# Convolution in two token halves, with the feed-forward of the first half interleaved, in a fused layer kernel

## The chip, the core and the metric

The kernel runs on one core of a Trainium2 chip. Its time is the device time of one execution in microseconds (us); the smaller, the better. A core has five engines that run their own instruction queues in order and meet only through semaphores: PE (TensorE, matrix products), ACT (ScalarE), DVE (VectorE), POOL (GpSimd) and SP (SyncE, which here issues nearly all DMAs). Matmul results land in PSUM, eight banks per partition, and have to be copied out ("evicted") to SBUF by ACT or DVE.

## The reference

Shapes: S = 2048 tokens, D = 640 channels, F = 1728 hidden features, bfloat16.

```python
k_shift = sum over t of k_pad[:, t:t + S, :] * shift_k[:, ks - 1 - t]      # 4 taps
kv = k_shift * v
y  = irfft(rfft(kv, 2S) * rfft(ssm_k, 2S))[:S] + kv * ssm_D                # causal, per channel
h  = x + layernorm(x) * y                                                  # x is A_q
h2 = h + (mish(layernorm(h) @ w1 + b1)) @ w2
```

Mish is h * tanh(softplus(h)). So there is a causal convolution over 2048 tokens in each channel, two layer norms, a gate and a feed-forward of 640 to 1728 to 640.

## The kernel before

**The convolution.** The transform of length 4096 is done as products on PE. Time is split as t = 16 t1 + t2. *Stage 1* (`stage1`, L500, matmuls L510 and L511) multiplies, for each group of channels, a 128 x 64 slice with a cosine and a sine table of 128 columns; the two write the two halves of the partitions. *Stage 2* (`s2_pe`, L527, matmul L539) has one 128 x 128 table per frequency f1 (128 of them, tile G), times 64 or 32 columns. Both run once for the filter (names s1k, s2k) and once for kv (s1v, s2v). G is not loaded: a compact table R (1 MB) is loaded (L473) and DVE spreads it by 16 masked products (`gb`, L483).

The filter is transposed on PE first (k1, L560). The shift with its four taps runs as small matmuls with diagonal matrices on 32 rows each (kspe, L586), from k loaded by transposing DMAs (d_kT, L476); DVE multiplies the result with v (L597). The filter's spectrum KP is also copied with the partition halves exchanged, by 20 DMAs of 256 KB (d_swap, L639), so that the complex product is two element-wise products on DVE (L720). The *inverse* is two steps: i1 (L731 and L732, two accumulating products per group, 20 evictions) and i2 (L782, six matmuls for a tile of 128 tokens, all 128 rows and columns in use).

**The rest.** For each of 16 token tiles: statistics of x (L676, L677), a reciprocal root on POOL (L422), the normalised x on ACT (lnx, L789), times the convolution out of PSUM (wb, L793), plus x (h, L797), statistics of h (L802, L803), the normalised h (dr, L812), five PE transposes (trpe, L819) and their eviction (trev). A unit of tokens (UNITS: 128, 128, 256, 512, 512, 512) then goes through the first product (m1pe, L845, 14 feature chunks of 128, the last half empty), Mish on ACT (hb, L851), the second product (m2pe, L861, 28 matmuls a tile), the addition of h (res, L870) and the output DMA (L873). Up to 24 filler matmuls (L830) keep PE running between i1 and the first unit.

**What sets the order.** The program lists operations with costs, dependences and priorities (table PRIO); `_schedule` (L145) plays them out on model engines, chooses ACT or DVE for each eviction and a pair of PSUM banks, and the instructions are emitted in the order of the modelled start. The evictions go through one helper, `ev` (L388; ACT is L390, DVE is L392). The feed-forward waits for the whole convolution: every i2 tile reads all of i1's output, and i1 comes after all products.

Of the kernel before, what the change touches and what calls it, by code (L numbers as in the profile page):

```python
# [11 lines left out]
ALU = mybir.AluOpType  # L12
# [4 lines left out]
S = 2048  # L17
# [4 lines left out]
NDG = 160  # L22
# [3 lines left out]
UNITS = [128, 128, 256, 512, 512, 512]  # L26
CHAIN = [80, 80.5, 81, 81.5] + [100.3, 100.31, 101.3, 101.31] + [102.3, 102.31, 102.32, 102.33] + [103.3, 103.31, 103.32, 103.33]
GRP_DC = [[0, 1], [2, 3], [4]]
GRP_DG = [(32 * g[0], 32 * g[-1] + 32) for g in GRP_DC]
NGRP = len(GRP_DC)  # L30
Q_KN = ("sp",) * NDC
Q_R = "sp"
Q_V = "sp"
Q_SWAP = "sp"
KTP = 16 + S
PRIO = {
    "k11": -197.031, "kv3": -192.001, "trev5": -189.16, "dr4": -188.917, "ln1_4": -185.4, "d_w2_8": -183.299, "i2pe1": -183.28, "d_w1_1": -182.827,
    "ln2s_14": -182.817, "ln1_11": -182.369, "ln1_13": -179.511, "wb7": -178.983, "dr0": -177.34, "lnx8": -174.207, "s1v4": -173.982,
    "ln1_9": -173.036, "ln1_15": -173.036, "h12": -173.025, "dr14": -173.025, "dr9": -172.894, "s2k0": -172.418, "ln2_15": -172.408, "h13": -172.023,
    "d_x1": -171.432, "ln2s_12": -170.801, "gb3": -167.776, "ln1_10": -166.532, "trpe6": -166.522, "trpe3": -165.629, "h11": -164.77,  # L40
    "ln2_0": -158.964, "kv2": -157.471, "s2k1": -157.461, "d_w1_4": -157.461, "ln1f6": -140.087, "d_kn0": -136.228, "h14": -87.6278, "h5": -84.944,
    "d_kn1": -84.3457, "h3": -84.0417, "wb11": -83.75, "dadd2": -79.55, "prod1": -75.932, "s1v3": -71.4952, "i2pe0": -68.0843, "ln1_6": -65.6205,
    "d_small": -63.7909, "i2pe3": -46.3801, "prod0": -44.976, "h1": -43.6934, "kv1": -39.0187, "ln1_14": -38.1351, "ln2_11": -38.1251,
    "lnx11": -36.0598, "d_R": -35.7363, "dadd0": -33.0275, "i2pe5": -33.0079, "wb1": -30.0642, "k10": -28.9847, "i2pe2": -28.8839, "h10": -28.7223,
    "d_t2m2": -27.8175, "kv4": -26.7596, "ks2": -24.7067, "kTpad": -24.6967, "trpe14": -18.2332, "ln2s_2": -18.2232, "ln1_8": -16.2738,
    "s2v1": -13.55, "wb14": 53.9493, "dr2": 56.1891, "trev11": 76.4003, "prod2": 76.4103, "trev2": 76.5744, "lnx12": 83.0874, "ln1f12": 84.6952,
    "ln2s_7": 84.9682, "i2pe7": 85.4105, "s1k1": 85.8777, "ln1s4": 86.1434, "lnx13": 86.1434, "ln2s_13": 86.1434, "d_w2_2": 86.2865, "wb12": 86.3538,
    "wb6": 88.7157, "trev9": 88.8047, "dr1": 89.3089, "h2": 90.4433, "dadd3": 91.1611, "lnx15": 91.1711, "d_x2": 91.1811, "wb10": 96.232,
    "trpe0": 97.2334, "d_w2_6": 97.2434, "gb2": 99.9385, "dadd4": 100.943, "c_diag": 102.191, "ln1_12": 103.577, "i10": 103.587, "s2v2": 103.597,
    "h8": 103.597, "lnx10": 103.607, "d_kn3": 104.126, "wb2": 106.246, "trpe2": 107.085, "h7": 107.848, "ln2_5": 107.903, "i2pe6": 108.973,  # L50
    "dr10": 110.068, "d_t2m3": 110.222, "k14": 111.266, "d_x3": 111.276, "ln2s_5": 111.611, "lnx4": 111.807, "d_b1": 112.158, "h4": 112.585,
    "s1k3": 112.595, "k13": 113.424, "dr15": 113.55, "ln2_13": 114.336, "i12": 114.475, "wb5": 114.476, "i2pe4": 114.485, "d_x0": 115.118,
    "d_w2_12": 115.124, "trev14": 115.124, "lnx9": 115.128, "lnx2": 115.378, "d_w1_0": 115.411, "trev12": 115.469, "ln1_5": 115.479, "ln1f0": 115.674,
    "d_w2_4": 115.88, "ln1s0": 116.071, "ln2s_11": 116.442, "d_kn4": 116.478, "ks3": 116.488, "s1k4": 116.498, "s1v2": 116.498, "trpe1": 116.508,
    "trev4": 116.686, "dr13": 117.267, "dr12": 117.27, "lnx3": 117.281, "ln2s_10": 118.476, "ln1f2": 120.706, "ln2s_4": 121.167, "trpe5": 121.177,
    "ln2_14": 121.46, "trev1": 121.47, "ln1s2": 121.577, "ln1f4": 121.587, "d_kn2": 122.535, "dr3": 123.819, "trev6": 124.987, "h6": 125.859,
    "ln2s_3": 126.587, "ln1f8": 126.597, "s2v0": 126.931, "ks0": 126.987, "d_v1": 127.413, "ln2_6": 127.672, "i2pe8": 127.672, "dr6": 127.682,
    "trev15": 128.067, "gb0": 128.252, "ln2_2": 129.397, "h0": 129.422, "dr5": 129.653, "dr11": 130.28, "ln2_3": 130.769, "wb15": 130.779,
    "gb1": 130.789, "d_v0": 132.33, "trev0": 132.596, "ln2_7": 133.484, "i2pe11": 135.983, "ln1s12": 137.388, "ln2s_9": 137.679, "ln2_1": 139.461,
    "d_t2m0": 140.202, "trpe7": 140.669, "kv0": 142.766, "trev13": 142.775, "ln2s_15": 144.326, "ks1": 144.336, "ln2s_1": 144.482, "ln2_8": 145.614,  # L60
    "trpe15": 145.919, "k12": 145.929, "dr8": 149.209, "lnx7": 150.735, "d_w2_10": 150.975, "trev8": 150.985, "wb4": 151.881, "trpe8": 152.822,
    "c_b1": 153.173, "s1k0": 154.561, "d_kT0": 155.252, "trev3": 155.262, "d_w1_3": 155.316, "dadd1": 155.326, "s1v1": 155.326, "trpe4": 155.336,
    "ln2_10": 155.388, "d_x6": 155.398, "ln1s8": 156.048, "ln1_1": 156.058, "lnx1": 156.078, "d_x7": 157.931, "ln1_3": 159.901, "d_swap2": 160.38,
    "wb0": 160.441, "i2pe9": 160.974, "d_x5": 160.984, "i2pe12": 163.067, "ln2s_6": 163.441, "d_kT1": 164.275, "trpe10": 165.151, "i2pe13": 167.089,
    "ln2_4": 169.091, "i2pe10": 169.366, "trpe13": 170.057, "wb13": 170.931, "ln1_0": 172.475, "trpe12": 172.485, "ln1_7": 172.852, "i2pe15": 173.706,
    "ln2s_8": 174.688, "trpe9": 175.572, "d_w1_2": 176.078, "i2pe14": 176.088, "trev10": 177.413, "ln2_9": 179.75, "s2k2": 181.125, "d_t2m1": 181.135,
    "dr7": 183.042, "s1v0": 184.508, "wb3": 187.188, "d_kT4": 193.464, "d_w2_0": 195.652, "s1k2": 196.175, "ks4": 196.195, "ln1s6": 198.464,
    "ln2s_0": 199.521, "ln2_12": 199.531, "trev7": 201.426, "i11": 202.634, "h9": 202.644, "d_kT2": 204.785, "d_x4": 207.553, "d_swap0": 209.773,
    "h15": 210.788, "wb8": 214.107, "lnx14": 217.331, "ln1_2": 217.341, "lnx5": 217.861, "lnx0": 219.423, "d_kT3": 222.092, "lnx6": 223.895,
    "trpe11": 227.243, "wb9": 230.005, "d_swap1": 230.845,  # L70
}

OFF_KP = 0
OFF_KPS = 40960
OFF_KN = OFF_KPS
OFF_KT = OFF_KN + 20480
OFF_G = OFF_KT + NDC * KTP * 2
OFF_B = OFF_G + 32768
OFF_V = OFF_B + 40960
OFF_KK = OFF_V + 20480  # L80
OFF_XA = OFF_KK + 8192
OFF_KVB = OFF_XA + 8192
OFF_END = OFF_KVB + 12288
OFF_KVB2 = OFF_KK
OFF_R = OFF_XA
OFF_W1 = OFF_G
OFF_W2 = OFF_KPS
OFF_LNHT = OFF_KP
OFF_UB0 = OFF_KP + 20480
OFF_UB1 = OFF_KPS + 17920  # L90
OFF_T2M = OFF_KVB
OFF_LNX = OFF_KVB + 8192
OFF_HC = OFF_XA
OFF_OB = OFF_XA + 3840

class _Ring:


# [3 lines left out]
_CELL = {}  # L102
# [8 lines left out]

class _Op:
    __slots__ = ("name", "opts", "deps", "allocs", "emit", "prio", "lat", "start", "finish", "eng", "done", "picks", "cap", "xbar")

    def __init__(self, name, opts, deps, allocs, uses, emit, prio, lat):
        self.name = name
        self.opts = opts if isinstance(opts, list) else [opts]
        self.deps = deps
        self.allocs = list(allocs)
        for rt in list(allocs) + list(uses):  # L120
            rt.users.append(self)
        self.emit = emit
        self.prio = prio
        self.lat = lat
        self.start = None
        self.finish = None
        self.eng = None
        self.done = False
        self.cap = 0.0
        self.xbar = False  # L130

_WIN = 0.3
_SEM = 0.18
_OWN = {"act": 0.1, "dve": 0.1}
_FIRST = 0.6
_LAST_BYTE = 1.6

def _stage(name):
    m = re.match(r"(k1|s1k|s2k|kp|ks|kv|s1v|s2v|x|prod|i1|gb|d_swap|c_diag|d_kn|d_kT|d_R|d_v)(?:pe|ev)?(\d*)(?:_.*)?$", name)
    if not m:  # L140
        return name
    st = {"kp": "s2k", "x": "s2v"}.get(m.group(1), m.group(1))
    return st + m.group(2)

def _schedule(ops):  # L145
    _CELL.clear()
    free = {}
    order = []
    cap_free = 0.0
    ring_free = {}  # L150
    ring_sent = {}
    ndeps = {id(o): len(o.deps) for o in ops}
    children = {}
    for o in ops:
        for d in o.deps:
            children.setdefault(id(d), []).append(o)
    bl = {}
    for o in reversed(ops):
# [768 lines left out]
```

## Time and profile before

| what | value |
|---|---|
| median of 3 runs | 244.1 us (242.97 to 246.27) |
| profiled execution, first to last instruction (the page names no other time of it) | 238.7 us |
| PE busy | 221.0 us (93%), 3266 matmuls |
| VectorE busy | 155.5 us (65%) |
| ScalarE busy | 139.5 us (58%) |
| GpSimd busy | 20.3 us (9%) |
| DMA | 25.52 MB, mean 107 GB/s |
| granted TensorE clock | 1.000 |

A row of busy time adds what an engine ran, overlaps within the engine counted once. In the rows of groups, "xN" is the number of instructions, "128x1024 bf16<-128x1024 f32" the output and the input (partitions x elements, type). The chain of waits is followed back from the last instruction; the timeline has start, duration, engine, line and operation, with the idle time before it in brackets. The largest groups are the evictions on ACT (L390, 78 of 1024 elements, 73.2 us), the second product (L861, 62.0 us) and the first (L845, 62.3 us). Matmuls are pipelined: the mean duration of one (L861: 299 ns) is longer than the distance from one to the next.

### The profile page before, as it was taken

How to read it: one execution, taken by the hardware profiler on the slowest of the kernel's cores; microseconds unless marked ns; L12 is line 12 of the kernel's file. 1: busy time of each engine (PE TensorE's matmuls, PEld its weight loads, DVE VectorE, ACT ScalarE, POOL GpSimd, SP SyncE). 2: the span in 40 equal slices, each digit the busy share in tenths (PEclk: the TensorE clock that was granted, in tenths of full speed). 3: DMA queues.
4: the chain of work that ended last, by engine and by line, in shares of the span. 5: the costliest groups of instructions: out<-in, count | busy, mean ns of one | idle time of the engine just before them, and what ended most of it. 6: DMA issues, size and time to landing. Idle time of an engine off the chain costs nothing.

```text
span 238.7 us, 7414 instructions
## 1 busy us (share of the span) xinstructions
PE 221.0 (93%) x3266; PEld 167.2 (70%) x3266; DVE 155.5 (65%) x318; ACT 139.5 (58%) x192; POOL 20.3 (9%) x39
## 2 busy tenths in 40 slices
PE   8888688988779999999999999999999999999993
PEld 3777577888779998698788764577744677545772
DVE  0998967899979998899999898584350332100121
ACT  2668676989998999589166456930156401366000
POOL 2500000000000003022311200210000000000000
PEclk9999999999999999999999999999999999999999
DMA  6999999806999797000000000001000001000001
GB/s 235 393 340 228 173 181 225 124 3 150 238 233 388 236 368 292 5 3 3 27 30 1 27 30 0 0 4 55 27 30 0 0 30 52 31 0 3 27 27 55
DMA packets 20049, 25.52 MB, mean 107 GB/s; under 512 B 11633, under 2 KB 15538, under 8 KB 19634
## 3 DMA queue, kind: packets, MB, share of 16 engines
q1 hardware_dynamic: 19760, 24.88, 37.5%
q8 instruction: 25, 0.41, 0.7%
q10 hardware_dynamic: 146, 0.18, 0.5%
q0 software_dynamic: 112, 0.01, 0.1%
q14 instruction: 6, 0.05, 0.1%
HBM read 14.57 MB, written 2.62 MB: 72 GB/s over the span
## 4 chain that ended last, share of the span: by engine, by line
PE 77%; ACT 10%; issue 4%; DVE 4%; DMA 3%; SPq 0%; ACTq 0%; DVEq 0%
PE banks L861 26%; PE banks L845 25%; ACT arena L390 9%; PE banks L539 6%; PE banks L731 4%; PE banks L732 4%; PE banks L782 3%; DMA arena<-tab_R 3%; PE banks L510 3%; PE banks L586 2%; DVE arena L392 2%; PE banks L819 2%; PE banks L560 1%; PE banks L830 1%; PE banks L511 1%
## 5 line engine op out<-in xcount | busy, mean ns | idle before, releaser
L390 ACT CAST arena<-banks 128x1024 bf16<-128x1024 f32 x78 | 73.2, 1046 | 16.3 <-PE banks L511 10.6
L845 PE MATMUL banks<-arena 128*128 128x512 bf16 (+2 forms) x420 | 62.3, 308 | 0.3 <-ACT arena L390 0.2
L861 PE MATMUL banks<-arena 128*128 128x320 bf16 x448 | 62.0, 299 | 0.2 <-DVE arena L793 0.2
L851 ACT ACTIVATE arena<-banks,b1s 128x512 bf16<-128x512 f32 (+2 forms) x84 | 43.5, 546 | 27.6 <-PE banks L845 25.5
L861 PEld LDWEIGHTS <-arena 128*128 128x128 bf16 x448 | 43.6, 98 | 17.1 <-issue 0.4
L845 PEld LDWEIGHTS <-arena 128*128 128x128 bf16 x420 | 35.3, 98 | 25.7 <-issue 0.7
L870 DVE TENSOR_TENSOR arena<-banks,arena 128x640 bf16<-128x640 f32 x16 | 13.2, 824 | 43.3 <-PE banks L861 43.2
L539 PE MATMUL banks<-arena 128*128 128x64 bf16 (+1 forms) x768 | 25.3, 188 | 4.6 <-ACT arena L390 2.9
L392 DVE CAST arena<-banks 128x1024 bf16<-128x1024 f32 x22 | 26.3, 1221 | 4.5 <-PE banks L511 2.2
L390 ACT COPY arena<-banks 128x640 bf16<-128x640 bf16 (+1 forms) x12 | 8.6, 746 | 32.7 <-PE banks L819 32.5
L539 PEld LDWEIGHTS <-arena 128*128 128x128 bf16 x768 | 23.3, 97 | 6.2 <-issue 5.1
L720 DVE TENSOR_TENSOR arena<-arena 128x1024 bf16<-128x1024 bf16 x40 | 24.8, 687 | 2.2 <-ACT arena L390 1.7
L510 PE MATMUL banks<-consts,arena 128*64 128x128 bf16 x320 | 21.3, 220 | 3.4 <-ACT arena L390 2.0
L511 PE MATMUL banks<-consts,arena 128*64 128x128 bf16 x320 | 21.6, 221 | 0.0
L511 PEld LDWEIGHTS <-arena 128*64 128x64 bf16 x320 | 18.4, 110 | 3.4 <-issue 3.2
L731 PE MATMUL banks<-consts,arena 128*128 128x128 bf16 x160 | 18.8, 219 | 1.3 <-DVE arena L392 0.9
L510 PEld LDWEIGHTS <-arena 128*64 128x64 bf16 x320 | 18.7, 110 | 1.7 <-issue 1.0
L732 PE MATMUL banks<-consts,arena 128*128 128x128 bf16 x160 | 18.7, 219 | 0.0
L732 PEld LDWEIGHTS <-arena 128*128 128x128 bf16 x160 | 15.6, 98 | 1.3 <-issue 1.0
L731 PEld LDWEIGHTS <-arena 128*128 128x128 bf16 x160 | 15.6, 98 | 0.6 <-issue 0.6
L789 ACT ACTIVATE arena<-arena,nmr_75,r1v 128x640 bf16<-128x640 bf16 x16 | 14.4, 926 | 2.6 <-DVE nmr_75 L684 1.4
L392 DVE COPY arena<-banks 128x1024 bf16<-128x1024 bf16 (+1 forms) x14 | 8.0, 598 | 11.8 <-PE banks L819 11.7
(47 smaller groups left out, 181.0 us busy)
## 6 DMA issues: line engine op xcount, KB each, us to landing
arena<-arena SPq DMA_DIRECT2D x20, 256.0 KB, 6.0
arena<-in_A_ssm_k_dram SPq DMA_DIRECT2D x5, 512.0 KB, 8.2
arena<-in_A_v_dram SPq DMA_DIRECT2D x2, 1280.0 KB, 15.4
arena<-in_A_q_dram SPq DMA_DIRECT2D x8, 320.0 KB, 5.6
out_dram<-arena SPq DMA_DIRECT2D x16, 160.0 KB, 1.8
arena<-in_B_w_dram SPq DMA_DIRECT2D x5, 432.0 KB, 8.4
arena<-in_B_w_dram SPq DMA_DIRECT2D x6, 320.0 KB, 4.8
arena<-tab_R SPq DMA_DIRECT2D x1, 1024.0 KB, 7.4
```

The lines of the kernel that those rows point to most:

```text
L390: clock.append(nc.scalar.copy(o, i))
L392: nc.vector.tensor_copy(o, i)
L510: nc.tensor.matmul(ps1[0:64, gl, :], lhs, fcfs_b[:, 0, :], start=True, stop=True)
L511: nc.tensor.matmul(ps1[64:128, gl, :], lhs, fcfs_b[:, 1, :], start=True, stop=True)
L539: nc.tensor.matmul(ps2[:, c0:c0 + nd], G_t()[:, f0 + fl, :], src[:, f0 + fl, :], start=True, stop=True)
L720: nc.vector.tensor_tensor(kp, x, kp, ALU.mult)
L731: nc.tensor.matmul(pz[:, gl, :], KP_t()[:, dg, :], a12_b[:, 0, :], start=True, stop=False)
L732: nc.tensor.matmul(pz[:, gl, :], KPS_t()[:, dg, :], a12_b[:, 1, :], start=False, stop=True)
L789: nc.scalar.activation(lnx.tile, xn_t()[:, t2, :], ACT.Identity, scale=r1v[:, t2:t2 + 1], bias=nmr1[:, t2:t2 + 1])
L845: nc.tensor.matmul(ph[:, 0:w], w1_t()[:, dc, fc * P:(fc + 1) * P], lnhT_t()[:, dc, c0:c0 + w], start=(dc == 0), stop=(dc == NDC - 1))
L851: nc.scalar.activation(ub_t[u % 2]()[:, fc, 0:w], rt.tile[:, 0:w], ACT.Mish, bias=b1s[:, fc:fc + 1], scale=1.0)
L861: nc.tensor.matmul(po[:, hf2 * 512:hf2 * 512 + 320], hb[:, fc, tl * P:(tl + 1) * P], w2_t()[:, fc, hf2 * 320:(hf2 + 1) * 320], start=(fc = ...
```

## The change

The file is rewritten in most places. What it does:

- **Two halves.** Tokens are cut in two windows of 1024. The transform has half the length (64 frequencies f1, NF, in place of 128; G has 64 tables). The filter has two windows of its spectrum (KA and KB), kv has two (XA and XB). Half 0 of the output is XA times KA; half 1 is XB times KA plus XA times KB. Stage 2 of the filter handles both windows in one matmul of 128 columns (64 for the last group), that of kv goes window by window (s2v, s2w).
- **Products.** prod (half 0) is one DVE instruction of 2048 elements that reads x twice through a repeated operand. Half 1 takes three such instructions per slice of channels (pu, pt, pa; 10 slices).
- **Swaps.** 10 DMAs of 256 KB for KA, then 40 of 128 KB for half 1's operands (d_swapr, d_swapk).
- **Order.** The feed-forward of tokens 0 to 1023 (units 0 to 4) is emitted between the products and inverse stage of half 1 (pu, pt, pa, i1b). Nine units of 128 or 256 tokens. There is no scheduler any more: `ORDER` is a string of all operations with engine and bank slot, in the order in which they are emitted.
- **i2.** Eight matmuls per tile, each on 64 rows and 64 columns, N = 320. A tile's partitions are two runs of 64 tokens, so x is loaded in 16 DMAs and out is stored in 34.
- **Stage-2 table.** G is loaded from DRAM in four DMAs of 512 KB (2 MB in all); the masked products are gone.
- **Transposes.** Tiles 0 and 1 keep PE transposes; tiles 2 to 15 are transposed by DMA (d_tr, on SP's queue).
- **m1.** In a unit of two tiles the last feature chunk (64 features) takes both tiles side by side on the two halves of the columns. The last tile's second product is split in 512 and 128 columns.
- **Statistics.** The addition of epsilon and the scaling move from DVE to POOL; some of the statistics of x may run on ACT (two activations with a sum), some of dr on ACT.
- **Gone:** fillers, paced DMAs.

The diff, cut to its core:

```diff
-UNITS = [128, 128, 256, 512, 512, 512]
+UNITS = [[0], [1], [2, 3], [4, 5], [6, 7], [8, 9], [10, 11], [12, 13], [14, 15]]
...
+ORDER = """
+d_consts:a d_kn0:s warmset:d d_small:v d_kn1:s pewarm:p:0 d_kn2:s d_kn4:s warm:a d_kn3:s d_v1:s w2zero:v d_G1:s d_G3:s kTpad:v d_G0:s d_kT1:s d_v0:s
+d_kT0:s d_kT3:s d_G2:s drow:p:1 c_diag:v d_kT2:s d_kT4:s dadd0:d d_t2m:s d_w2_13b:s k1pe0:p:2 dadd1:d k1pe1:p:3 k1ev0_1:d k1ev0_0:a dadd2:d
...
+ln2_0:d lnx1:a s2wpe1_2:p:3 ln1_4:d ln2s_0:v d_swapk1_0:s s2wev1_2:a d_swapk2_0:s d_w2_9:s wb1:d d_swapk0_1:s s2wev1_0:a ln1s4:v s2wpe0_0:p:3
+d_swapk0_0:s d_swapk2_1:s dr0:d i2pe2:p:0 d_w2_0:s s2wev0_0:a h1:d d_swapr2_0:s trpe0:p:0 d_swapr2_1:s wb2:d d_swapr0_0:s trev0:a d_swapr0_1:s
+d_w2_3:s ln2_1:d lnx4:a d_w2_6:s m1pe0_1:p:1 d_swapk1_1:s m1pe0_3:p:2 d_swapr4_0:s m1pe0_2:p:3 hb0_1:a ln1_3:d d_swapr3_1:s m1pe0_7:p:0 ln2s_1:v
...
+"""
+def _ordered(ops):
+    by_name = {o.name: o for o in ops}
...
+    for tok in ORDER.split():
+        name, e, *slots = tok.split(":")
+        o = by_name.pop(name)
+        o.eng = engines[e]
+        for rt, k in zip(o.allocs, slots):
+            rt.slot = rt.ring.slots[int(k)]
...
-    DMA("d_R", 1.05e6, lambda e: ENG_Q[Q_R].dma_start(R_t().rearrange("p f q -> p (f q)"), dram["R"]), w=["R"], prio=1.015, q=Q_R)
+    for c in range(4):
+        DMA(f"d_G{c}", 524e3, (lambda e, c=c: nc.sync.dma_start(view(OFF_G + c * 4096, 2048), dram["G"][:, c * 2048:(c + 1) * 2048])),
+            w=[iv(OFF_G + c * 4096, 4096)], prio=1.015 + 0.0001 * c)
-                nc.vector.tensor_scalar(dst, src, mask[:, dl:dl + 1], None, ALU.mult)
...
+    def stage2(prefix, grp, offs, w0, prio):
...
+                for fl in range(nf):
+                    nc.tensor.matmul(ps2[:, fl * n:(fl + 1) * n].rearrange("p (w g) -> p w g", w=nw),
+                                     G_t[:, f0 + fl, :], src[:, :, f0 + fl, :], start=True, stop=True)
...
+    for s in range(NSL):
+        po = OFF_PK + (s % 4) * 4096
+
+        def prod(e, s=s, po=po):
+            nc.vector.tensor_tensor(strided(po, [1024, 2], [1, 1024]), strided(OFF_XA + s * 2048, [0, 2], [1, 1024]),
+                                    strided(OFF_KS + s * 2048, [(OFF_KA - OFF_KS) // 2, 2], [1, 1024]), ALU.mult)
...
+    def second(s, prio):
...
+        swap(f"d_swapr{s}", OFF_KA + s * 2048, ks0, 2048, prio - 0.5)
+        swap(f"d_swapk{s}", OFF_KB + s * 2048, ks1, 2048, prio - 0.5)
+        OP(f"pu{s}", ("dve", _dve2(2048)), r=[iv(OFF_XB + s * 2048, 2048)], w=[ia, ib], prio=prio,
+           emit=lambda e: nc.vector.tensor_tensor(k0, strided(OFF_XB + s * 2048, [0, 2], [1, 1024]), k0, ALU.mult))
+        OP(f"pt{s}", ("dve", _dve2(2048)), r=[iv(OFF_XA + s * 2048, 2048)], w=[i0, i1], prio=prio,
+           emit=lambda e: nc.vector.tensor_tensor(k1, strided(OFF_XA + s * 2048, [0, 2], [1, 1024]), k1, ALU.mult))
+        OP(f"pa{s}", ("dve", _dve2(2048)), r=[ia, ib], w=[i0, i1], prio=prio,
+           emit=lambda e: nc.vector.tensor_tensor(k1, k1, k0, ALU.add))
+        inverse("i1b", s, (lambda w: view(OFF_KB + s * 2048 if w == 0 else ks1, 1024)), [i0, i1], OFF_KB, prio)
...
-                    nc.tensor.matmul(py[:, 4 * d0:4 * d1], t2m_t()[:, t2, ri, :], zb_t[grp]()[:, ri, t2, :], start=(ri == 0), stop=(ri == 1),
-                                     skip_group_check=True)
+            for ri in range(2):
+                for j in range(2):
+                    for ee in range(2):
+                        rows = slice(64 * ee, 64 * ee + 64)
+                        nc.tensor.matmul(py[64 * j:64 * j + 64, ee * 512:ee * 512 + 320].rearrange("p (s c) -> p s c", s=NSL),
+                                         t2m_t[rows, 8 * j + i, ri, :], z[rows, :, ri * 16 + 8 * j + i, :], start=(ri == 0), stop=(ri == 1))
...
+    def rsqrt(o, v, n, c=1.0):
+        nc.gpsimd.tensor_scalar(v, v, c, EPS, ALU.mult, ALU.add)
         nc.gpsimd.tensor_tensor(o, v, mhalf[:, 0:n], ALU.pow)
...
+            DMA(f"d_tr{t}", 164e3, lambda e: nc.sync.dma_start_transpose(lnh, hc), r=[iv(ho, 1280)], w=[liv], prio=pr - 1, rate=150e3)
...
+                    if two:
+                        for j in range(2):
+                            nc.tensor.matmul(ph[64 * j:64 * j + 64, 0:P], w1_t[:, dc, fc * P:fc * P + 64], lnht[:, dc, j * P:(j + 1) * P],
+                                             start=(dc == 0), stop=(dc == NDC - 1))
...
+            for c0, c1 in pieces:
+                for j in range(2):
+                    DMA(f"d_out{t}_{c0}_{j}", 128 * (c1 - c0), (lambda e, j=j, b=b, i=i, ob=ob, c0=c0, c1=c1: nc.sync.dma_start(ov[0, b, j, :, i, c0:c1], ob[64 * j:64 * j + 64, c0:c1])),
+                        r=[iv(oo + c0 * 2, (c1 - c0) * 2)], prio=pr + 5, rate=340e3)
...
-    order = _schedule(ops)
+    order = _ordered(ops)
```

In ORDER a token is an operation, its engine (p PE, a ACT, d DVE, v POOL, s SP) and its bank slots.

## The prediction

> **What bounds the kernel now.** I read the page's slices first, then busy time in stretches of 10 us, then the chain of work in order of time, then the timelines of single engines for the pitch of back-to-back instructions. The slices show two kernels in one:
>
> ```profile
> PE   8888688988779999999999999999999999999993
> DVE  0998967899979998899999898584350332100121
> ACT  2668676989998999589166456930156401366000
> DMA  6999999806999797000000000001000001000001
> GB/s 235 393 340 228 173 181 225 124 3 150 238 233 388 236 368 292 5 3 3 27 30 1 27 30 0 0 4 55 27 30 0 0 30 52 31 0 3 27 27 55
> ```
>
> A slice is 6 us. Up to slice 16 (about 100 us) VectorE and ScalarE are full and the DMAs too for the first 40 us, while PE has holes. After it PE is full, DMA empty, and VectorE fades. The stretches (PE, PEld, DVE, ACT, POOL busy us, then clock, DMA share, GB/s) give sizes:
>
> ```profile
> 20.00:30.00 10.00, 6.83 (x224) 6.22 (x219) 8.32 (x14) 6.99 (x8) 0.00 (x0) 1.00 1.20 167
> 50.00:60.00 10.00, 9.08 (x317) 8.62 (x314) 9.47 (x14) 9.76 (x12) 0.00 (x0) 1.00 0.45 98
> 80.00:90.00 10.00, 10.00 (x239) 9.60 (x236) 9.83 (x23) 10.00 (x12) 0.55 (x5) 1.00 0.89 295
> 110.00:120.00 10.00, 10.00 (x97) 7.82 (x95) 9.40 (x26) 4.83 (x11) 2.84 (x5) 1.00 0.05 18
> 180.00:200.00 20.00, 20.00 (x135) 12.50 (x133) 5.13 (x10) 6.57 (x10) 0.55 (x1) 1.00 0.05 17
> ```
>
> Clock 1.00 throughout, so no term below needs a correction for it. The chain of waits (start, us, what) is PE alone from 101.5 us on; its rows price everything in the feed-forward:
>
> ```profile
> 120.53 7.64 PE banks L845 x70
> 128.17 0.28 PE banks L819 x5
> 128.45 0.55 PE banks L782 x6
> 129.00 3.80 PE banks L861 x28
> 234.91 0.82 DVE arena L870
> ```
>
> So a first product over 256 tokens is 7.64 us, a transpose of a tile 0.28, its inverse product (L782) 0.55, its second product 3.80. The timelines price the rest by pitch, not by the mean, which contains overlap:
>
> ```profile
> 74.98 16.61 ACT L390 CAST arena<-banks 128x1024 bf16<-128x1024 f32 x18
> 75.48 6.10 DVE L720 TENSOR_TENSOR arena<-arena 128x1024 bf16<-128x1024 bf16 x10
> 18.96 3.48 DVE L392 CAST arena<-banks 128x1024 bf16<-128x1024 f32 x3
> 27.72 2.48 DVE L597 TENSOR_TENSOR arena<-banks,arena 128x512 bf16<-128x512 f32 x4 [0.58 <-issue]
> 5.46 25.24 SPq L476 DMA_TRANSPOSE arena<-in_A_k_dram  x4
> ```
>
> An eviction of 1024 is 0.94 on ACT and 1.17 on DVE; a product of 1024 is 0.61, so one of 2048 is 1.22; a pair of shift products is 1.24. The median is 244.1 us and the span 238.7; I carry the 5.4 us between them over unchanged.
>
> **Change part by part.** I cut the written order at the first feed-forward matmul (m1pe0_1) and at the first one of half 1 (m1pe5_0), and add each engine's rows in each part.
>
> Part A, to the first feed-forward matmul. Removed: 16 mask products (0.53 each on DVE), half of the inverse stage's 20 evictions, half the spectrum products, 24 fillers. DVE: 25 evictions x 1.17 = 29.3, 10 shift pairs 12.4, 10 products x 1.22 = 12.2, 7 statistics x 1.13 (rows L676 and L677 without the added epsilon) = 7.9, 7 evictions of transposes x 0.62 = 4.3, the tiles' first operations 4.5: 70.6. ACT: 65 x 0.94 + 3 x 0.96 + 4 normalisations x 0.83 + 0.6 = 67.9. PE: 60.4. DVE and ACT bound it together, as now.
>
> Its front is bound by DMA. 6.3 MB of plain loads (filters, table R, v) were in by about 19.5 us: 2 us of start and 360 GB/s. Then transposed loads hold the queue (9.2 us for the last three of the four: 3.07 each, while GB/s falls to 167), and the first shift product ran at 24.5, so a landing takes 1.2 more. The change's table G is 2.10 MB in four loads, not 1.05 MB, all on SP's queue. Ahead of the third shift product (kspe2) stand 7.34 MB of loads and four transposes: 2 + 20.4 + 12.3 + 1.2 = 36 us; DVE's 26.3 us of work before it, from its start at 6.4 us and at the filling found below, end at 34.7, and kspe0's own load (28.2 against 26.7) adds 1.5. I take 36.6. Behind kspe2 in PE's queue stand s1v and s2k matmuls that ACT and DVE wait for, so all three engines lose these 1.9 us. The 44.3 us of DVE work left run at the filling that DVE had from 50 to 90 us (37.5 of 40) and from 100 to 140 (37.2 of 40), 0.93: 47.6. Part A ends at 84.2, against 101.5 now. The start-up of the first tile (chain now: 95.4 to 101.5) is hidden beside the s2w evictions, 7.1 us of DVE work after i2pe0; without that cover it would cost 6.
>
> Part B, feed-forward of half 0 beside half 1's products. DVE: pu, pt, pa 30 x 1.22 = 36.6, 15 statistics 17.0, wb, h, dr, res and one eviction 19.6: 73.2. PE: two single units 8.2, three double units x 7.38 = 22.1 (13 x 0.546 + 5 x 0.0585: the last 64 features of two tiles side by side), 8 second products 30.4, 10 i1b x 0.89 = 8.9 (16 matmuls at 0.0555, pitch of L731 and L732), 8 i2, one transpose 0.3. ACT: about 59. At 0.93 DVE takes 78.7.
>
> i2 goes from 6 matmuls to 8 on quarters of the array, a form no row shows. Bounds: 8 x 320 columns one after the other, by L861's 0.1357 each, 1.09 us; four at a time 0.27. L510 and L511, on two halves of the columns, keep the full pitch in pairs, and L586, on four row groups, runs 76 in 1.4; I take 0.27. Changing the layout costs too: the last pair of the s1 form starts at 54.28, the first L586 at 54.54, where the pitch inside is 0.055, and L539 starts 0.15 after the last L511 at 56.47. I add 0.12 a change, 0.24 per i2 and per packed m1: i2 0.51, PE in B 8.2 + 22.1 + 30.4 + 8.9 + 8 x 0.51 + 0.3 + 0.7 = 74.7, still under DVE's 78.7. At 1.09 it would be B 79.4 and 2.3 more in C. Without these drains part C would be 1.9 lower and the sum 232.6. [...]
>
> DMA transposes replace 14 of 16 PE transposes and their evictions: PE saves 14 x 0.28 = 3.9, ACT and DVE 14 evictions of 0.4 to 0.7. Price of one, 160 KB: between 0.33 us on SP's queue (an output of that size, landing 1.8) and 3.07 (L476, 512 KB; landing 5.1 to 7.1). By bytes 0.96. SP's queue in B holds 27 swaps of at most 1.06, 8 transposes of at most 3.07, 14 outputs and 8 loads at 0.35: at most 61 of 78.7, so it is not full, but everything stands in order: a swap waiting for pa or i1b holds the transposes behind it. The rows have transposes at 171 GB/s beside plain loads at 360. [...]
>
> The statistics' epsilon and scaling move to POOL: now 0.154 + 0.585 + 0.152 over two engines, then three POOL instructions, 0.8 (small ones as a memset, 0.1) to 1.76 (all as L422). 32 chains are at most 56 us of POOL's 230; longer by at most 0.9 each, hidden behind DVE's queue. Rows of half 1 swapped in 40 smaller transfers, x in 16, outputs in 34: DMA is idle there now.
>
> Part C, from m1pe5_0: PE four units 29.5, eight second products 30.4, four i2 2.0, four packed ends 1.0: 62.9. DVE 18 and ACT 25 hide. The end is 0.22 for the last 128 columns, two issues 0.7, landing and close 2.4: 3.3, where now 3.8.
>
> Sum: 84.2 + 78.7 + 62.9 + 3.3 = 229.1 span, + 5.4 = **234.5 us**. PE's own work falls from about 205 to 196; the rest of the gain is that the eviction-bound stage is shorter.
>
> **Rivals.** 1: *Three full engines wait on each other in B.* PE 74.7 and DVE 73.2 with ACT 59 in fixed orders; now only two were full at a time after 100 us. From 10 to 50 us DVE was 0.85 full (34 of 40). At 0.85 B takes 86.1: 241.9; with A too (88.7), 246.4. Against it: 50 to 90 us, all three at 0.9 and more. 2, *slower: late transposes.* PE takes its queue in order; if the seven double units each find their transposed tiles late, PE stands. 249 is reached at 2.1 us per unit; with 3 us, half of L476's landing, 255.5. For it: SP's order above. Against: most double units have 4 to 7 us of other PE work between transpose and first use. 3: *products of 2048 with a repeated operand lose the fast form*: at the pace of the DVE cast (1.17 per 1024) they are 2.3, +11 in A, +33 in B: 282; it costs 2% from 0.36 an instruction. L720's strided runs kept 0.61, so 3 in 100. That the overlap does not happen at all is excluded: the order is written out.
>
> **Numbers.** Forecast 0.62 with its own range 226 (fillings of 0.97 in A and B give 229.4, no drains 227.5, no wait at kspe0 226.0) to 239; rival 1 0.23 (239 to 249); rival 2 0.12; rival 3 0.03. Range 226 to 249 leaves out 0.15 above and some 0.04 below. Two per cent, what a measurement can tell, is 239.2 to 249.0: faster 0.62, same 0.23, slower 0.15.
>
> **What would show it.** First feed-forward matmul at 84 (A), kspe2 waiting for a transposed load near 36, DVE about 0.93 full to 163, then PE full to the end; products of 2048 at 1.2; i2 near 0.5 per tile. Wrong if the first m1 of a double unit waits for a DMA, if evictions run under 0.9 full, or if i2 takes 1.1.

## The result and the profile after

The changed kernel takes 283.5 us (median of 4 runs, 280.3 to 285.0) against 244.3 us of the kernel before on the same chip: ratio 1.156, 95% interval 1.145 to 1.168. It is slower, where 234.5 us and "faster" were predicted. The profiled execution has a span of 278.6 us and took 280.3, the shortest of the four.

The slices of the changed kernel (7 us each now), with the granted clock:

```profile
PE   8874777888898597349969465886999999999992
DVE  1655675798889980679467903389692753110121
ACT  2884574768798985066757425167755762158100
PEclk9999997999999979958999977798999999999999
DMA  7999973903994299342341143410224034110111
```

Where the kernel before had PE full from about 100 us on, PE now has holes from slice 14 to slice 28 (91 to 195 us), and VectorE (0 in slices 16 and 24) and ScalarE (0 in 17, 1 in 26) have them too. No engine stays full there: three engines wait in turn. The clock, 1.00 throughout before, falls at the holes, to 0.5 in slice 18.

The stretches by stage, in the columns used before (PE, PEld for PE's loads of weights, DVE, ACT, POOL busy us, clock, DMA share, GB/s). The first is the start-up in front of part B, the second is part B as the prediction cut it, from the first feed-forward matmul to the first one of half 1:

```profile
84.20:97.50 13.30, 9.10 (x190) 7.23 (x187) 13.09 (x24) 12.49 (x16) 6.66 (x14) 0.98 0.32 75
97.50:210.20 112.70, 85.78 (x819) 66.50 (x819) 70.22 (x109) 61.32 (x122) 37.90 (x65) 0.88 0.39 89
```

The work of the two evicting engines in part B is what was predicted: VectorE 70.2 us (73.2 predicted), ScalarE 61.3 (59). PE has 85.8 busy us (74.7 predicted), at a clock of 0.88. But VectorE fills 0.62 of the 112.7 us, where 0.93 was taken. By parts (kspe2 lies within part A):

| | predicted | measured | miss |
|---|---|---|---|
| third shift product starts (kspe2) | 36.6 | 48.2 | +11.6 |
| A: first feed-forward matmul at | 84.2 | 97.5 | +13.3 |
| B | 78.7 | 112.7 | +34.0 |
| C and the end | 66.2 | 68.4 | +2.2 |
| span | 229.1 | 278.6 | +49.5 |

Some of the longest waits (who waited for whom: us in total, times, longest) show who stands and for what:

```profile
...
PEld L626 <- DVE arena L659: 15.0, 5, 8.2
DVE arena L659 <- DMA arena<-arena: 14.6, 3, 6.3
...
DVE arena L657 <- DMA arena<-arena: 12.8, 3, 9.5
...
ACT arena L350 <- DVE arena L659: 9.5, 2, 5.6
```

L655, L657 and L659 are the new products of half 1 (pu, pt and pa), "DMA arena<-arena" are here the swaps, L626 the inverse matmuls, L350 ScalarE's evictions. VectorE waits for swaps, and PE and ScalarE wait for VectorE. The first hole, in VectorE's timeline (start, us, instruction, idle time before it and its releaser):

```profile
104.07 0.44 DVE L721 TENSOR_SCALAR arena<-arena,mv,r 128x640 bf16<-128x640 bf16 x1
113.97 1.23 DVE L657 TENSOR_TENSOR arena<-arena 128x2048 bf16<-128x2048 bf16 x1 [9.46 <-DMA arena<-arena]
115.11 0.49 DVE L703 TENSOR_TENSOR arena<-arena 128x640 bf16<-128x640 bf16 x1
```

This is pt0, the product of slice 0. It stands 9.5 us for a swap, and behind it in VectorE's queue stand h3, a statistics block and everything that ScalarE and PE need from them. Its cause is not in the profile but in the program's own waits. The first line below is pt0 as built, the other two are the same product split in two instructions (the first experiment):

```
L657 TensorTensor arena<-arena 128x2x1024 [waits DMAHW4_49,DMAHW5_49,DMAHW3_49,DMAHW6_49,DMAHW2_49,DMAHW7_49,DMAHW1_49,DMAHW0_49]

L656 TensorTensor arena<-arena 128x1024 [waits DMAHW5_49,DMAHW4_49]
L656 TensorTensor arena<-arena 128x1024
```

One instruction writes two runs of 1024 that lie 25600 elements apart (slice 0 in KB and its copy in a slot of KS2). The automatic synchronisation takes such an operand as the whole stretch from the first run to the end of the second. In that stretch lie the slots into which the transfers d_swapr of slices 0 to 4 land, none of which pt0 needs, and pt0 waits on eight queues of landings and not two. I call this a false wait. Laid against what each instruction really reads and writes, the waits of the built program and the times of the trace give an estimate of the idle time that only false waits cause: some 40 us on VectorE, 22 on ScalarE and 8 on PE. No view has this estimate, but its largest part stands in rows: VectorE's products wait 32.3 us for swaps, 14.6 and 12.8 us in the rows above and 4.9 for L655. In the kernel before it is next to nothing on the three computing engines. Operands of many short runs close together show no such cost: in e8 below, whose evictions write 64 runs of 8, hardly any idle time from false waits is left by this estimate.

### The profile page after: what moved, and what is told of

Read it like the earlier page. It is cut to its first block, busy times and chain, and to the rows that moved or that the text cites. A ratio compares the mean times of both kernels' runs of the same rounds, so it can differ in the third digit from the quotient of the medians.

```text
span 278.6 us, 7571 instructions
## 1 busy us (share of the span) xinstructions
PE 224.8 (81%) x3262; PEld 180.1 (65%) x3262; DVE 157.9 (57%) x237; ACT 158.7 (57%) x254; POOL 57.2 (21%) x113
## 4 chain that ended last, share of the span: by engine, by line
PE 40%; DVE 17%; DMA 17%; ACT 10%; issue 5%; SPq 4%; POOL 3%; DVEq 0%; ACTq 0%
PE banks L794 15%; PE banks L764 12%; DMA arena<-arena 8%; ACT arena L350 7%; DVE arena L352 6%; PE banks L482 5%; DMA arena<-in_B_w_dram 4%; DVE arena L659 3%; DMA arena<-in_A_q_dram 2%; DVE arena L655 2%; DMA arena<-in_A_ssm_k_dram 2%; PE banks L626 2%; DVE arena L657 2%; PE banks L459 2%; SPq L518 2%
## 5 line engine op out<-in xcount | busy, mean ns | idle before, releaser
L350 ACT CAST arena<-banks 128x1024 bf16<-128x1024 f32 x75 | 73.0, 1018 | 42.2 <-PE banks L482 13.4
L768 ACT ACTIVATE arena<-banks,b1s 128x256 bf16<-128x256 f32 (+1 forms) x126 | 52.4, 444 | 31.1 <-PE banks L764 24.0
L764 PE MATMUL banks<-arena 128*128 128x256 bf16 (+1 forms) x595 | 65.3, 269 | 5.2 <-ACT arena L350 5.2
L794 PE MATMUL banks<-arena 128*128 128x320 bf16 (+2 forms) x448 | 65.3, 306 | 4.9 <-DVE arena L799 2.5
L764 PEld LDWEIGHTS <-arena 128*128 128x128 bf16 x595 | 53.7, 102 | 14.6 <-issue 7.8
L794 PEld LDWEIGHTS <-arena 128*128 128x128 bf16 x448 | 44.0, 100 | 24.1 <-issue 5.2
L626 PE MATMUL banks<-consts,arena 128*128 128x128 bf16 x320 | 24.4, 241 | 20.2 <-DVE arena L659 9.9
L626 PEld LDWEIGHTS <-arena 128*128 128x128 bf16 x320 | 21.8, 109 | 22.6 <-DVE arena L659 15.0
L482 PE MATMUL banks<-arena 128*128 128x64 bf16 (+2 forms) x576 | 25.2, 198 | 12.9 <-DVE arena L352 6.5
L482 PEld LDWEIGHTS <-arena 128*128 128x128 bf16 x576 | 22.4, 99 | 15.6 <-issue 13.9
L799 DVE TENSOR_TENSOR arena<-banks,arena 128x640 bf16<-128x640 f32 x15 | 12.2, 818 | 34.9 <-PE banks L794 34.9
L377 POOL TENSOR_SCALAR mv<-mv 128x1 f32<-128x1 f32 x32 | 12.0, 374 | 91.1 <-DVE mv L708 56.2
L659 DVE TENSOR_TENSOR arena<-arena 128x2048 bf16<-128x2048 bf16 x10 | 12.2, 1225 | 15.0 <-DMA arena<-arena 14.6
L657 DVE TENSOR_TENSOR arena<-arena 128x2048 bf16<-128x2048 bf16 x10 | 12.2, 1224 | 13.1 <-DMA arena<-arena 12.8
L698 DVE TENSOR_TENSOR arena<-banks,arena 128x640 bf16<-128x640 f32 x16 | 12.9, 810 | 10.7 <-PE banks L689 5.9
L695 ACT ACTIVATE arena<-arena,nmr,r1v 128x640 bf16<-128x640 bf16 x16 | 14.4, 921 | 5.2 <-DVE arena L703 2.8
L719 ACT ACTIVATE arena<-arena,nm,r 128x640 bf16<-128x640 bf16 x7 | 6.4, 918 | 18.2 <-POOL nm L715 15.2
```

Of the source, the lines that this page charges most:

```text
L350: nc.scalar.copy(o, i)
L482: nc.tensor.matmul(ps2[:, fl * n:(fl + 1) * n].rearrange("p (w g) -> p w g", w=nw), G_t[:, f0 + fl, :], src[:, :, f0 + fl, :], start=True, ...
L626: nc.tensor.matmul(pz[:, gl, :], src_ap(w)[:, gl * 128:(gl + 1) * 128], a12_b[:, w, :], start=(w == 0), stop=(w == 1))
L657: emit=lambda e: nc.vector.tensor_tensor(k1, strided(OFF_XA + s * 2048, [0, 2], [1, 1024]), k1, ALU.mult))
L659: emit=lambda e: nc.vector.tensor_tensor(k1, k1, k0, ALU.add))
L695: emit=lambda e: nc.scalar.activation(lnx, x_t(t), ACT.Identity, scale=r1v[:, t:t + 1], bias=nmr1[:, t:t + 1]))
```

## Experiments

All ratios are to the kernel before on the same chip; [ ] is the 95% interval. One chip each had e1 to e4, e5 and e6, e7 to e9, e10 and e11, e12 and e13, so that times compare directly within these groups and ratios across them. The edits are shown shortened.

**e1: products in one-run instructions.** Each pu, pt and pa becomes two instructions of 1024 with the same data and the same place in the order.

```diff
-  tensor_tensor(k0, strided(OFF_XB + s * 2048, [0, 2], [1, 1024]), k0, mult)
+  for o, x, y in zip(h0, [OFF_XB + s * 2048] * 2, h0):   # h0 = (KA slice, its slot)
+      tensor_tensor(view(o, 1024), view(x, 1024), view(y, 1024), mult)
```

> The three products of half 1 (pu, pt, pa), each one instruction over two runs of 1024 that lie 40 to 61 KB apart, become two instructions over one run each; nothing else changes. Theory A, false waits: the synchronisation takes an operand of two distant runs as everything between them, so a product waits for every swap landed or under way in that stretch and holds up i1b's evictions; 37 us of DVE idle stand before such waits in the trace of the changed kernel, most of them on the path between 110 and 190 us. A expects 245 to 258 us. Theory B, GpSimd's chains of small instructions (0.19 to 1.1 and 0.55 to 1.5 us when a long product runs beside them) hold up the tiles: no change, 278 to 285. Theory C, the swaps themselves arrive late behind DMA transposes in SP's queue: no change, 278 to 285.

251.7 us, ratio 1.038 [1.028, 1.047], where the changed kernel has 1.156: some 30 us come back for 30 more instructions. Part B is 82.8 us in place of 112.7:

```profile
99.40:182.20 82.80, 77.85 (x818) 61.30 (x818) 70.60 (x139) 60.38 (x122) 34.57 (x65) 0.96 0.51 121
```

VectorE at the place of the hole, and its products' waits for swaps over the whole span:

```profile
104.68 0.44 DVE L725 TENSOR_SCALAR arena<-arena,mv,r 128x640 bf16<-128x640 bf16 x1
105.04 1.29 DVE L656 TENSOR_TENSOR arena<-arena 128x1024 bf16<-128x1024 bf16 x2
106.24 0.48 DVE L707 TENSOR_TENSOR arena<-arena 128x640 bf16<-128x640 bf16 x1
```

```profile
DVE arena L656 <- DMA arena<-arena: 4.4, 3, 2.2
```

The pair that is pt0 now runs 0.36 us after L725's start, without a wait: its data was there. The waits of the products for swaps, 14.6, 12.8 and 4.9 us for L659, L657 and L655, have become 4.4. This settles the bulk of part B.

**e2: all two-run operands split**, in the front as well: evictions of stages 1 and 2 and the stage-2 matmuls of the filters, one window each.

```diff
-  nc.tensor.matmul(..., G_t[:, f0 + fl, :], src[:, :, f0 + fl, :], ...)      # both windows
+  for w in range(nw):
+      nc.tensor.matmul(..., G_t[:, f0 + fl, :], ws[w][:, f0 + fl, :], ...)
```

> As e1, and also prod, the stage-1 evictions, the filter's stage-2 matmuls and its evictions written per window, so that no operand spans two windows: 60 evictions of 1024 become 120 of 512, 128 matmuls of 128 columns become 256 of 64. Theory A: part A, which lost some 12 us to such waits between 16 and 65 us, gets these back, less 60 times about 0.1 us for the extra instructions shared by two engines: 4 to 10 us below e1, 236 to 250. Theories B and C: as the changed kernel or slower by the extra instructions, 280 to 290.

250.9 us, ratio 1.037 [1.023, 1.052]: no gain on e1. The first feed-forward matmul comes at 96.6 (99.4 in e1), so the front's false waits seemed to cost little. What took their place shows in PE's timeline, where one group of 16 equal transposes (L508) breaks off after four:

```profile
33.01 0.44 PE L508 MATMUL banks<-consts,arena 128*128 128x128 bf16 x4
36.56 1.45 PE L508 MATMUL banks<-consts,arena 128*128 128x128 bf16 x12 [3.11 <-issue]
```

Inside such a group the program has no wait, so I take the instructions themselves to have been missing for these 3.11 us. e7 comes back to this.

**e3: the statistics' small operations back from GpSimd to VectorE**, against the theory that GpSimd is the cause.

```diff
-  nc.gpsimd.tensor_scalar(v, v, c, EPS, mult, add)
+  nc.vector.tensor_scalar(v, v, c, EPS, mult, add)      # and the two products with the mean
```

> One part of the change undone alone: epsilon, scaling and the mean's product go back from GpSimd to DVE (three to one GpSimd instruction per statistic). Theory B: the four waits of 3 to 5 us on GpSimd's chains shrink to about 1 each and the time falls to 262 to 272. Theory A: these chains stand behind DVE's false waits, so 278 to 286. Theory C: the same.

291.3 us, ratio 1.202 [1.161, 1.242], no faster than the changed kernel's 1.156, and the first feed-forward matmul comes at 106.4. The edit also gives VectorE 62 more instructions, so it is no clean test; but e1 gets its 30 us back with GpSimd's chains left as they are, and with that the theory falls as the main cause.

**e4: the swaps left out** (the 40 transfers that exchange the row halves of half 1 are not made, so half 1 is computed from other data).

```diff
-  swap(f"d_swapr{s}", OFF_KA + s * 2048, ks0, 2048, prio - 0.5)
-  swap(f"d_swapk{s}", OFF_KB + s * 2048, ks1, 2048, prio - 0.5)
```

> Leaves out work: the 40 swap transfers of half 1 are not issued, so half 1's products read what lies in their place. Theory C: all waits for them go, 240 to 255. Theory A: the waits on transfers go as well, but false waits among products, i1b's evictions and PE stay: 255 to 268. Theory B: 275 to 285.

255.2 us, ratio 1.053 [1.017, 1.088], on the border between what theories A and C had, so that it does not decide between them. The waits are on swaps, then. But e1, which makes all of them, is no slower (its four runs, 250.5 to 252.1, lie under e4's two, 253.5 and 256.9, on the same chip): it is not the swaps that cost, it is waiting for the wrong ones.

**e5 and e6: windows side by side.** Part A was still 15.2 us over the prediction in e1. For channel groups 0 and 1 the two windows of the filters' first stage are put next to each other, so that evictions write and matmuls read one run; no instruction is added. e5 has this and e1's products, e6 this alone.

```diff
-  dst = strided(OFF_B0 + d0 * 128, [10240, 2], [nd, NF], [1, nd])
+  dst = strided(OFF_BW[grp], [nd, 2 * NF], [1, nd])          # groups 0, 1 of the filters
```

> e1 (products split into two one-run instructions) and, in the front, the two windows of the filters' first stage laid side by side for the first two channel groups, so that an eviction writes and a stage-2 matmul reads one run; no instruction is added anywhere. What is left of the miss after e1 is part A: first feed-forward matmul at 99.4 us where 84.2 was predicted, third shift product at 49.0 where 36.6 was. Theory A (false waits between ScalarE's and VectorE's evictions and the stage-2 matmuls, about 12 us of idle time between 16 and 48 us): third shift product at 40 to 44, first feed-forward matmul at 91 to 95, time 243 to 248. Theory C (the front is bound by the loads, whose transposes end near 38 us, and by the fetch of PE's instructions behind them, seen in e2 as two PE gaps of 2.5 and 3.1 us that wait for nothing): third shift product stays at 46 to 49, time 249 to 252.

> The layout of e5 on the changed kernel alone: the products of half 1 keep their two far runs. Theory A: the false waits of the product stage stay (34 us in part B), so only the front's share comes back: 274 to 280, and the first feed-forward matmul at 90 to 94 where it is 97.5. Theory C: 281 to 285, first feed-forward matmul at 96 to 98.

e5: 246.6 us, ratio 1.016 [1.002, 1.030]; third shift product at 44.8 (49.0 in e1), first feed-forward matmul at 95.4. The time is as theory A had it, the two places just beside its bounds. e6: 280.0 us, 1.156 [1.140, 1.173], third shift product at 45.4, first feed-forward matmul at 96.5, where theory C had it: alone it is worth almost nothing. Part B is 113.5 us, no shorter than the changed kernel's, and of the 2.7 us won at the third shift product 1.0 is left at the first feed-forward matmul; why is not shown.

**e7: plain loads.** e5 with the key tensor loaded untransposed (the same bytes to the same place; what is computed from it is other).

```diff
-  nc.sync.dma_start_transpose(kT_t[:, dc, 16:KTP], A_k[0, :, dc * P:(dc + 1) * P])
+  nc.sync.dma_start(kT_t[:, dc, 16:KTP], A_k.rearrange("b (p a) d -> p (b a d)", a=16)[:, dc * 2048:(dc + 1) * 2048])
```

> e5 with the five loads of the key tensor as plain loads of the same bytes to the same place (the transposition is left out, so what is computed from it is other than the reference). In e5 PE stands 1.6 us at 22.1 and 2.4 us at 34.5 in the middle of a group of equal matmuls, where nothing but its instructions can be missing, and a fetch of 16 KB of them (at 21.2 and 34.2 in e2) lies before each while the DMA share is 1.0 to 1.2. Theory C (PE's instructions come late behind the loads): with the loads done by about 28 us in place of 38 the second gap goes and the half clock after it, third shift product at 40 to 42 in place of 44.8, first feed-forward matmul 3 to 4 us earlier, time 242 to 245. Theory D (the gaps have another cause, or what they cost is hidden behind the evictions): both gaps stay or the time stays at 246 to 248.

Third shift product at 40.6, first feed-forward matmul at 91.7, as theory C had it, and both gaps of e5 (PE stood at 22.1 and at 34.5) are gone. First e5, then e7, in the same stretch:

```profile
20.00:30.00 10.00, 6.80 (x127) 5.96 (x131) 5.87 (x6) 6.57 (x8) 0.00 (x0) 1.00 1.05 251
30.00:40.00 10.00, 7.61 (x243) 7.00 (x236) 6.93 (x11) 5.21 (x6) 0.00 (x0) 0.89 1.18 231
```

```profile
20.00:30.00 10.00, 7.90 (x189) 7.03 (x190) 7.12 (x6) 7.35 (x8) 0.00 (x0) 1.00 1.00 403
30.00:40.00 10.00, 8.64 (x229) 7.63 (x228) 9.09 (x12) 7.74 (x8) 0.00 (x0) 1.00 0.16 41
```

The DMA share falls from 1.18 to 0.16 in the fourth ten microseconds, since 403 GB/s are moved and not 251, and PE, VectorE and ScalarE all do more. Yet the time is 247.1 us, 1.011 [1.001, 1.021]: two waits for the second weights at the first second product give a part back (part B 84.8, 2.1 longer):

```profile
103.64 0.57 PE L813 MATMUL banks<-arena 128*128 128x320 bf16 x3 [2.23 <-DMA arena<-in_B_w_dram]
106.67 3.63 PE L813 MATMUL banks<-arena 128*128 128x320 bf16 x13 [2.46 <-DMA arena<-in_B_w_dram]
```

**e8 and e9.** e8 is e5 with the remaining two-run evictions split (no more matmuls); e9 is e8 with the loads d_w2_3 and d_w2_6 moved ahead of four swaps in SP's queue.

```diff
-  ev(e, dst, rt.tile.rearrange("p (f w g) -> p w g f", f=nf, w=nw))
+  for w, off in enumerate(offs):                                             # e8
+      ev(e, strided(off + d0 * 128 + f0 * 2, [NF, nd], [1, nf]), rt.tile.rearrange("p (f w g) -> p w g f", f=nf, w=nw)[:, w])
-  ... d_w2_0:s ... d_swapr2_0:s ... d_swapr0_1:s d_w2_3:s ... d_w2_6:s ...
+  ... d_w2_0:s d_w2_3:s d_w2_6:s ... d_swapr2_0:s ... d_swapr0_1:s ...       # e9, in the order
```

> e5 with the evictions that still write two far runs (stage 1 of the values and of the last channel group, stage 2 of the filters) as two instructions of 512 each; no matmul is added, other than in e2. An eviction then costs 0.06 us more. Theory A: 5.6 us of idle time of ScalarE, VectorE and PE before 62 us still come from such waits; two to four of them come back: first feed-forward matmul at 91 to 94 (95.4 in e5), time 242.5 to 245.5. If they are hidden or eaten by the longer evictions: 246 to 248.

> e8 with the last two loads of the second weights ahead of four swaps in SP's queue. In e5 the first second product waits 1.9 us (107.2 to 109.5) for one of them, and PE's clock is half for the 3.4 us after it, about 3.6 us together. Theory: part B is 79 to 80.5 us in place of 82.8, time 2 to 4 us under e8: 239 to 243, level with the kernel before or 2% under it. If the delayed swaps hold up VectorE's products by as much: as e8.

e8: 246.1 us, 1.009 [1.004, 1.015], span 243.2, first feed-forward matmul at 94.3, third shift product at 42.5. e9: 246.0 us, 0.999 [0.988, 1.010], part B 82.1. Neither came out as hoped. In e8 hardly any idle time from false waits is left on the engines, but the pauses of PE of 0.3 us and more that the profile marks "issue", which means that nothing it shows was waited for, add up to 6.5 us, where they are 2.8 in e5 and none in the changed kernel. I read this as PE running into its missing instructions as it waits less for evictions. In e9 the wait for the weights is gone, but in e8's profile it was already down to 0.2 us (1.9 in e5), so there was little to remove; the waits of VectorE's products for swaps go from 2.6 to 5.1 us in part B, which was the second half of what was expected.

**e10: e9 with e7's plain loads** (the transposition left out), to close the account of part A.

> e9 (products split, windows side by side, evictions split, second weights first) with the plain loads of e7 (the transposition is left out). It closes the account of part A. If the miss there is the false waits plus PE's instructions late behind the loads, both are now mostly gone: third shift product at 38 to 40.5 (36.6 predicted), first feed-forward matmul at 87 to 90.5 (84.2 predicted), part B 80 to 82, time 237 to 242. If something else holds part A, or part B gives it back as in e7: 243 to 247.

240.1 us, 0.993 [0.989, 0.997]; third shift product at 39.7, first feed-forward matmul at 89.8, part B 82.7. With false waits mostly gone and the loads plain, part A misses the prediction by 5.6 us and not by 13.3. PE still pauses for 3.9 us, by the count used for e8.

**e11, e12, e13: a shorter GpSimd chain.** e11 is e9 without the scaling and the epsilon of the statistics (32 instructions left out). e12 is e9 again and e13 is e11 again, on one chip.

```diff
-  nc.gpsimd.tensor_scalar(v, v, c, EPS, mult, add)
```

> e9 without the scaling and the epsilon in the statistics (left out: 32 small GpSimd instructions), so that GpSimd's chain per tile is two instructions and not three. Theory B (GpSimd's instructions, stretched beside VectorE's long products, sit on the path of part B): part B 79 to 80.5 us where e9 has 82.1, time 1.5 to 3 us under e9. If they hide behind VectorE's queue: part B and the time as in e9, within 1 us.

> e9 once more, now beside the kernel with the short chain on one chip: 0.995 to 1.005 of the kernel before.

> The short chain (scaling and epsilon left out) once more, on the chip of the run before it. Its profile showed part B 4 us shorter, its time against the kernel before did not (0.9986 against 0.9988, on two chips). Theory B: 1 to 2% under the run beside it, and part B again at 78 to 80 against 81 to 83. If part B only varies from run to run: within 0.5% of it.

e11: 243.4 us, 0.999 [0.993, 1.004], part B 78.2. e12: 245.9, 1.016 [1.010, 1.022], part B 81.9. e13: 243.4, 1.005 [1.001, 1.010], part B 81.5. On one chip the short chain is 2.5 us, 1%, faster, and the intervals just touch; but part B of e13's profile is no shorter than e12's, and e11's was. So a gain of about 1% is likely, its place is open. e9 and e12 are one kernel and came out at 0.999 (a ratio that rests on three runs) and 1.016: two measurements on two chips differ by that much, and the mended versions that compute everything (e8, e9) are level with the kernel before within it. None beats it by 2%.

The milestones of the profiled executions together (us):

| | kspe2 | first feed-forward matmul | B | C and end | span |
|---|---|---|---|---|---|
| predicted | 36.6 | 84.2 | 78.7 | 66.2 | 229.1 |
| changed kernel | 48.2 | 97.5 | 112.7 | 68.4 | 278.6 |
| e1 | 49.0 | 99.4 | 82.8 | 68.1 | 250.3 |
| e5 | 44.8 | 95.4 | 82.8 | 68.1 | 246.3 |
| e7 | 40.6 | 91.7 | 84.8 | 68.1 | 244.7 |
| e8 | 42.5 | 94.3 | 81.1 | 67.8 | 243.2 |
| e10 | 39.7 | 89.8 | 82.7 | 67.8 | 240.3 |

Each row is one execution, and its places vary. In e8, e9, e11, e12 and e13 nothing differs ahead of kspe2, and it comes at 42.5 to 45.8; the first feed-forward matmul comes at 93.4 in e9 and 97.4 in e12, the same kernel. So steps of 3 or 4 us in part A are rough, and smaller ones, such as that from e5 to e8, say nothing. The 30 us of part B are far outside this.

## Why the prediction was wrong

**The failed step** is "At 0.93 DVE takes 78.7", and with it "the filling that DVE had from 50 to 90 us" in part A. A filling was carried over from the kernel before to instructions of another shape. The kernel before had no operand of two far runs that could meet a swap; the change put one into every product of half 1, next to 40 swaps that land in between, and into the filters' evictions. The removal of that one property (e1) brings back 29.9 of the 34.0 us that part B missed. What remains in e1 is a filling of 0.85 (70.6 of 82.8 us), the number that rival 1 had; its time for B, 86.1, is 3.3 us too long, since VectorE's work is 2.6 us less than taken, and the forecast's 78.7 is 4.1 too short. So, false waits apart, the filling is rival 1's and the time lies between the two. Rival 1's total, 241.9 with A as predicted, also needs part A at 84.

**Part A.** The prediction's "I take 36.6" for kspe2 failed by 11.6 us. It took 0.93 for VectorE's work in the front too, although its own rows gave 0.85 for the kernel before from 10 to 50 us; VectorE in fact filled 0.49 of the stretch from 20 to 30 us in e1 and 0.59 in e5. False waits between the two evicting engines and the stage-2 matmuls are some 4 us of it (e1 to e5), the loads and what they delay, PE's late instructions among it, another 4 (e5 to e7); what the rest is stays open. The later part of A was nearly right: from kspe2 to the first feed-forward matmul 49.3 us where 47.6 was taken.

**The priced instructions held.** Rows of the changed kernel, busy us and mean ns of one:

```profile
L659 DVE TENSOR_TENSOR arena<-arena 128x2048 bf16<-128x2048 bf16 x10 | 12.2, 1225 | 15.0 <-DMA arena<-arena 14.6
L657 DVE TENSOR_TENSOR arena<-arena 128x2048 bf16<-128x2048 bf16 x10 | 12.2, 1224 | 13.1 <-DMA arena<-arena 12.8
...
L655 DVE TENSOR_TENSOR arena<-arena 128x2048 bf16<-128x2048 bf16 x10 | 12.0, 1208 | 5.3 <-DMA arena<-arena 4.9 <-ACT arena L350 0.2
```

A product of 2048 takes 1.21 to 1.22 us (1.22 taken), so rival 3 is out: its time, 282, is near the measured one by chance, its reason is not the reason. The idle column of the same rows holds what was missing. Eight matmuls of i2 (L689) have 0.47 us in PE's timeline, where 0.51 was taken, with 0.24 for the two changes of layout that the prediction calls drains (what PE does in them no row shows):

```profile
137.84 0.47 PE L689 MATMUL banks<-arena 64*64 64x320 bf16 x8
```

**Part C** was right in PE's work (62.9 us from its first matmul to the end of the last, 62.9 predicted); the end is 2 us longer, since the last tile leaves in four transfers that one queue issues in 2.6 us, not two in 0.7.

**Rival 2**, late transposes, did not decide: the holes are VectorE's waits. In the changed kernel two transposing DMAs stand in SP's queue from 110.4 for 10.7 us (L739), after VectorE's hole and, I take it, because of it. Of SP's queue the prediction said "everything stands in order": the right worry at the wrong place, since it was the products and not the transposes that stood behind the swaps.

**What was looked at and what was not.** The list of marks to watch had the first feed-forward matmul at 84 and VectorE at 0.93; both showed the failure at once. What the prediction did not do was to ask, of each instruction whose shape changes, which other writes lie between its runs. The kernel's text shows it: a step from a slice of KB to its slot ks1 between two runs, and swaps with their targets in between.

**Small slips in the sums** decide nothing: an eviction on ACT is 0.92 by the pitch of the row shown (16.61 us for 18) and not 0.94; the front's own terms give 36.0 or 36.2 and not 36.6; PE's three parts add to 198.0 and not 196; rival 3's +11 and +33 give 278.5, and 282 only when divided by 0.93.

## What to carry to other kernels

When two instructions are fused into one whose operand has two runs far apart, list everything that is written or read between the runs: with automatic synchronisation the fused instruction may wait for all of it, and what fusing saves is little (VectorE is busy for 157.9 us with the fused products and for 158.3 with e1's). Look at the built program's waits and compare their number with what the data needs; place buffers that one instruction touches side by side. A filling measured on one set of instructions is no price for another set: treat it as the least certain term, and give its failure a rival of its own.

## What the runs showed of the hardware

**Instructions come by DMA too.** They are fetched in packets of 16 KB (25 of them in the changed kernel); I take this queue for PE's, which has 6524 of the 7571 instructions recorded:

```profile
q8 instruction: 25, 0.41, 0.6%
```

PE pauses up to 3.1 us where nothing shown is waited for: 8.2 us in sum in e2, 6.5 in e8, 4.2 in the kernel before (pauses of 0.3 us and more), and with shorter loads (e7) the two early ones of e5, at 22.1 and 34.5, vanish (the profile puts the second down to VectorE, and the sums leave it out). In e8 such a packet starts at 21.6, 44.8 and 51.9 us, and PE stands from 22.4, 45.5 and 52.3, for 1.6, 2.0 and 2.5 us. The DMA is not full each time (share 1.06, 1.06 and 0.28 around them), and not every packet brings a pause: the changed kernel has 25 and no such pause. That the pauses come from the fetch is argued from their place and e7, not seen directly.

**PE's clock fell to 0.5 at its holes.** The clock by stretches of the changed kernel:

```profile
110.00:120.00 10.00, 3.15 (x22) 2.05 (x21) 5.89 (x10) 0.99 (x2) 2.89 (x4) 0.88 0.37 49
120.00:130.00 10.00, 7.88 (x48) 5.54 (x49) 7.99 (x14) 6.14 (x10) 5.65 (x9) 0.61 0.39 87
```

From 117.5 on, inside PE's hole of 7.9 us at 113.5, the clock is 0.5 for 10.2 us, and it falls to 0.5 for 3.4 us at six other places, each inside a pause of PE or up to 1.4 us after one; these pauses are 0.9 to 4.3 us long. Part B's PE work is 85.8 busy us at a clock of 0.88 where 74.7 was predicted (77.9 at 0.96 in e1). Not every pause does it: the clock falls at one of 1.9 us in e5 at 107.5, but one of 2.5 us in the changed kernel at 140.4 and one of 2.5 us in e8 at 52.3 leave it at 1.00. What decides it was not shown.

**GpSimd's small instructions took longer beside VectorE's products.** GpSimd's timeline while VectorE runs three products back to back (117.7 to 121.4), then beside its other work:

```profile
119.06 1.10 POOL L377 TENSOR_SCALAR mv<-mv 128x1 f32<-128x1 f32 x1
120.24 1.53 POOL L378 TENSOR_TENSOR r1v<-mv,mhalf 128x1 f32<-128x1 f32 x1
121.88 0.27 POOL L616 TENSOR_SCALAR nmr<-mv,r1v 128x1 f32<-128x1 f32 x1
124.86 0.19 POOL L377 TENSOR_SCALAR mv<-mv 128x1 f32<-128x1 f32 x1 [2.71 <-ACT arena L607]
125.13 0.55 POOL L378 TENSOR_TENSOR r1v<-mv,mhalf 128x1 f32<-128x1 f32 x1
```

The same two instructions take 1.10 and 1.53 us beside the products and 0.19 and 0.55 without. The chain of three takes 3.1 us the first time and 1.2 the second; the prediction had 0.8 to 1.76. What the stretching costs no run isolates; one instruction less in each chain (e12 to e13) is worth about 1%.
